# Attention and a mixture of experts on one core: k loaded two rows at a time, even rows in front of odd ones

## The chip, the core and the metric

The kernel runs on one core of a Trainium2 chip. The metric is the device time of one execution in microseconds (us), as the median of a few runs. Five engines each work through a program of their own, in order: TensorE (PE; its weight loads are shown apart as PEld), VectorE (DVE), ScalarE (ACT), GpSimd (POOL) and SyncE (SP, which issues nearly all DMA transfers). The engines meet only at semaphores. An instruction that waits holds up everything behind it in the program of its engine.

## The reference

The output is that of a block-causal attention followed by a layer of eight experts with a capacity.

```python
# q, k, v: (8 batches, 8 heads, 576 rows, 64) float32
scores = q @ k^T / sqrt(64)          # a query block of 64 rows sees key blocks up to its own
attn = softmax(scores)               # maximum taken off, masked places drop out
o = attn @ v                         # (8, 8, 576, 64)
x = o.transpose(0, 2, 1, 3).reshape(4608, 512)

logits = x @ w_gate                  # (4608, 8)
# pairs (token, expert) in falling order of logit; each expert takes at most 576 tokens
for e in range(8):
    out[mask_e] = relu(x[mask_e] @ w1[e]) @ w2[e]      # 512 -> 1024 -> 512
```

For the softmax the order of the keys in a row of scores has no meaning: the maximum and the sum run over all of them. The product with v needs the weights back in the order of the rows of v.

## The kernel before

**Stages.** The first stage is the attention with the logits, up to about 340 us of the profiled span. Then come the routing of the tokens and the experts, with PE products for the most part. The change is in the first stage alone.

**Units.** A unit n (0 to 31) is two heads of one batch, and a pair of units u = n // 2 is four heads. Loads, splits and transposes are done by pairs, scores and softmax by units. Pair 0 is handled in two halves and goes through PE transposes; pairs 1 to 15 go through DMA transposes.

**The path of k for one pair.** (1) `load_qk` (L246) brings 4 x 576 = 2304 rows of 64 float32 into the tile `kn`, 128 partitions by 18 chunks by 64: row 128c + p lies on partition p in chunk c. Each row is a run of 256 bytes in memory. There are two such tiles for k and two for q. (2) `split` makes two float16 parts of it in two halves of nine chunks each: the high part is a cast on ACT or DVE (L280, L278), the low part is the difference on POOL or DVE (L287). Both go into `k2` (`NQ=1`, one buffer). (3) A DMA transpose issued by SP (L324) turns `k2` into `kT`: partitions 0 to 63 hold one part and 64 to 127 the other, columns are the 2304 rows. (4) `swap` (L337, DVE) copies one part onto the other half of the partitions in `kS`, 1152 columns for each unit. (5) `scores` (L358, PE) multiplies: for each query block i it needs w = 64(i + 1) columns of keys. q goes the same way up to its transpose. Products of `kT` and of `kS` are added in PSUM, and the two heads of a unit go to partitions 0 to 63 and 64 to 127.

**Softmax of a unit.** The nine query blocks are taken in three groups (`GROUPS`), each in two banks of PSUM (1024 columns): group 0 holds blocks 8 and 6 with 576 and 448 columns, group 1 blocks 7, 5 and 1, group 2 blocks 4, 2, 3 and 0. DVE takes the maximum of each block (L376), ACT the exponentials with their sum into the tile `P` (L384), POOL multiplies with the reciprocal of the sum (L406). `transpose` turns `P` on PE (L431) with copies by ACT or DVE (L412, L414) into `PT`, and `values` multiplies with v (L466). A matmul writes one bank, so block 8 is cut into pieces of 512 and 64 columns.

**Other transfers of a pair.** v comes in five transfers (L261 four times, L264), together 576 KB. Results are transposed by DMA from `XT` to `XR` (L483) and written to `x` in memory (L490), 576 KB each per pair on average. So for each pair seven transfers of 576 KB go through SP: loads of k, q and v, transposes of q, k and XT, and a write.

**What sets the order.** Every function above is a generator that hands its next step to a planner (`Sched`) with an engine, a cost and the events that it waits for. The planner picks the step that can start first by its own clock, with priorities, and so fixes the program of each engine when the kernel is built. For DMAs the cost is given to `sc.dma(...)` in nanoseconds; these numbers shift the planned order on all engines, and move nothing on the chip by themselves. SP's program is in order: a transpose that waits for the low parts holds up the loads behind it.

Of the kernel before, what the change touches and what calls it, by code (L numbers as in the profile page):

```python
# [11 lines left out]
AF = mybir.ActivationFunctionType  # L12
# [148 lines left out]
class Attn:  # L161

    GROUPS = [[(8, 0), (6, 576)], [(7, 0), (5, 512), (1, 896)], [(4, 0), (2, 320), (3, 512), (0, 768)]]
# [72 lines left out]
    def load_qk(s):  # L236
        nc, sc = s.nc, s.sc
        for u in range(s.N // 2):
            b, hp = s.bh(2 * u)
            step = 2 if u else 1  # L240
            for i in range(0, 2, step):
                for nm, src in (('k', s.k), ('q', s.q)):
                    yield s.QE, 50, 'hw', ('sp', nm, 2 * (u - s.NB) + 1), ('ti', u - s.LQ)
                    if i == 0:
                        s.d[nm, u] = s.wp.tile([P, 18, s.D], F32, tag=nm + 'n', name=f"{nm}n{u}", bufs=s.NB)
                    s.ld(s.QE).dma_start(out=s.d[nm, u][:, 9 * i:9 * (i + step)],  # L246
                                         in_=src[b, 2 * (hp + i):2 * (hp + i + step)].rearrange("h s d -> (h s) d").rearrange("(c p) d -> p c d", p=P))
                    sc.dma(1638 * step, ('ld', nm, 2 * u + i))
# [3 lines left out]
    def load_v(s):  # L252
        nc, sc = s.nc, s.sc
        for u in range(s.N // 2):
# [3 lines left out]
            for h in range(4):  # L258
                if h:
                    yield s.VE, 50, 'hw'  # L260
                s.ld(s.VE).dma_start(out=t[:, 0:4, h], in_=s.v[b, 2 * hp + h, :512].rearrange("(c p) d -> p c d", p=P))  # L261
                sc.dma(728)
            yield s.VE, 50, 'hw'
            s.ld(s.VE).dma_start(out=t[:64, 4], in_=s.v[b, 2 * hp:2 * hp + 4, 512:].rearrange("h p d -> p h d"))  # L264
            sc.dma(364, ('ld', 'v', u), 625)

    def split(s, nm):
# [3 lines left out]
        for n in range(s.N):  # L271
# [4 lines left out]
            a, b = s.d[nm, u][:, 9 * i:9 * i + 9], t2[:, 9 * i:9 * i + 9]  # L276
            if sc.eng == D:
# [47 lines left out]
            sc.dma(2016 if u else 1008, ('tr', nm, n), 625, True)  # L325
# [5 lines left out]
    def swap(s):  # L331

        nc, sc = s.nc, s.sc
        for n in range(s.N):
            u, i = n // 2, n % 2
            yield D, 520, ('tr', 'k', n), ('s', 2 * (u - s.TB) + 1)
            nc.vector.tensor_copy(s.kS[u % s.TB][64:, 9 * i:9 * i + 9], s.d['kT', u][:64, 9 * i:9 * i + 9])  # L337
            sc.set(('sw', n))

    def scores(s):  # L340
        nc, sc = s.nc, s.sc
        for n in range(s.N):
            for g, G in enumerate(s.GROUPS):
                first = True
                for i, o in G:
                    w = 64 * (i + 1)
                    for a in range(0, w, 512):
                        e = min(w, a + 512)
                        yield T, 2 * ((e - a) / 2.4 + 27), Shape(2), ('tr', 'q', n), ('sw', n), 'S' if first else None
                        if first:  # L350
# [3 lines left out]
                        A, K1, K2 = [x[:, 9 * (n % 2):9 * (n % 2) + 9].rearrange("p c t -> p (c t)").rearrange("p (h t) -> p h t", h=2)  # L354
                                     for x in (s.d['qT', n // 2], s.d['kT', n // 2], s.kS[n // 2 % s.TB])]
                        for K, st in ((K1, True), (K2, False)):
                            for h in range(2):
                                nc.tensor.matmul(ps[64 * h:64 * h + 64, o + a:o + e], lhsT=A[:, h, 64 * i:64 * i + 64],  # L358
                                                 rhs=K[:, h, a:e], start=st, stop=not st)
# [3 lines left out]
                sc.add(s.softmax(n, g, tk, ps), s.PS, sc.now + 200)  # L363

# [706 lines left out]
```

## Time and profile before

| | |
|---|---|
| median of 3 runs | 801.75 us (799.38 to 802.38) |
| the profiled execution | 801.04 us, of which the span from first to last instruction is 799.3 us |
| granted PE clock, mean | 0.962 |
| busy in the span | PE 710.1 us, DVE 593.2, ACT 534.8, POOL 463.7 |
| transposes of P (L431) | 800 matmuls, 104.7 us busy |
| products with v (L466) | 792 matmuls, 97.4 us busy |
| scores (L358) | 640 matmuls of kT, 87.8 us, and 640 of kS, 80.9 us |
| exponentials (L384) | 288, 149.2 us busy |
| maxima (L376) | 288, 126.5 us busy |

The 1.8 us between the span and the time of the execution lie around the first and the last instruction. Busy times of different engines lie beside one another, so they cannot be added. A share of DMA can be over 1, since the times of packets overlap. In lists of groups the columns are line, engine, operation, what is written and read, shapes and count, then busy time in us, mean ns of one, and idle time before with its releaser.

### The profile page before, as it was taken

How to read it: one execution, taken by the hardware profiler on the slowest of the kernel's cores; microseconds unless marked ns; L12 is line 12 of the kernel's file. 1: busy time of each engine (PE TensorE's matmuls, PEld its weight loads, DVE VectorE, ACT ScalarE, POOL GpSimd, SP SyncE). 2: the span in 40 equal slices, each digit the busy share in tenths (PEclk: the TensorE clock that was granted, in tenths of full speed). 3: DMA queues.
4: the chain of work that ended last, by engine and by line, in shares of the span. 5: the costliest groups of instructions: out<-in, count | busy, mean ns of one | idle time of the engine just before them, and what ended most of it. 6: DMA issues, size and time to landing. Idle time of an engine off the chain costs nothing.

```text
span 799.3 us, 18655 instructions
## 1 busy us (share of the span) xinstructions
PE 710.1 (89%) x6301; PEld 463.5 (58%) x6301; DVE 593.2 (74%) x2487; ACT 534.8 (67%) x1450; POOL 463.7 (58%) x511
## 2 busy tenths in 40 slices
PE   5698889999988889913998999999999999999995
PEld 3565556667756657701644756647557475574752
DVE  6999879998989888788887977969687683720210
ACT  5798878989878778533845859495875847392210
POOL 5787778988888776412314337484571916773001
PEclk9989999999999999955999999999999999999998
DMA  9969999999999998544308048291945719871001
GB/s 193 180 134 194 228 185 191 216 179 212 199 181 214 200 191 168 119 96 143 128 14 296 22 161 218 86 274 43 269 121 191 166 52 257 286 159 41 21 15 44
DMA packets 286992, 125.62 MB, mean 157 GB/s; under 512 B 251568, under 2 KB 270000, under 8 KB 286896
## 3 DMA queue, kind: packets, MB, share of 16 engines
q1 hardware_dynamic: 281008, 105.55, 60.5%
q0 software_dynamic: 5888, 18.88, 7.9%
q8 instruction: 49, 0.80, 0.4%
q14 instruction: 47, 0.39, 0.2%
HBM read 71.32 MB, written 18.87 MB: 113 GB/s over the span
## 4 chain that ended last, share of the span: by engine, by line
PE 49%; DVE 22%; DMA 14%; ACT 5%; POOL 5%; issue 3%; SPq 1%; POOLq 0%; DVEq 0%; ACTq 0%
PE h L978 21%; PE y L1003 15%; DMA kT<-k 7%; DVE m L376 6%; PE psb L466 3%; PE psb L358 3%; PE psb L431 3%; POOL P L406 2%; DVE kS L337 2%; DMA raw<-in_moe_w_dram 2%; ACT P L384 2%; PE y L1007 2%; DMA xg<-x,ix 1%; DVE jk L724 1%; DVE PT L414 1%
## 5 line engine op out<-in xcount | busy, mean ns | idle before, releaser
L406 POOL TENSOR_TENSOR P<-P,m 128x576 f32<-128x576 f32 (+8 forms) x287 | 209.0, 762 | 57.3 <-DVE m L398 35.0
L978 PE MATMUL h<-X,W 128*128 128x320 f16 (+3 forms) x1536 | 194.9, 286 | 0.0
L384 ACT ACTIVATE P<-psb,m 128x576 f32<-128x576 f32 (+8 forms) x288 | 149.2, 543 | 31.3 <-DVE m L380 28.0
L978 PEld LDWEIGHTS <-W 128*128 128x128 f16 x1536 | 142.0, 98 | 42.7 <-issue 3.3
L1003 PE MATMUL y<-W,HH 128*128 128x512 f16 x512 | 152.7, 380 | 0.0
L899 POOL TENSOR_TENSOR W<-raw,W 128x1024 f16<-128x1024 f32 x56 | 118.4, 2137 | 39.1 <-ACT W L897 37.1
L376 DVE TENSOR_REDUCE m<-psb 128x1 f32<-128x576 f32 (+8 forms) x288 | 126.5, 480 | 3.5 <-PE psb L358 3.4
L431 PE MATMUL psb<-mident,P 128*128 128x128 f32 x800 | 104.7, 278 | 15.2 <-DVE XT L451 6.1
L994 POOL DMA_INDIRECT out_dram<-yo,ix x40 | 39.1, 978 | 114.9 <-ACT yo L986 79.5
L431 PEld LDWEIGHTS psb<-mident,P 128*128 128x128 f32 x800 | 86.0, 141 | 28.7 <-POOL P L406 10.3
L358 PE MATMUL psb<-kT,qT 128*64 128x512 f16 (+7 forms) x640 | 87.8, 298 | 14.9 <-DMA kT<-k 7.0
L466 PE MATMUL psb<-PT,V 128*64 128x448 f32 (+5 forms) x792 | 97.4, 388 | 1.2 <-ACT PT L412 0.9
L358 PEld LDWEIGHTS <-qT 128*64 128x64 f16 x1280 | 66.4, 113 | 53.7 <-issue 36.5
L1003 PE MATMUL y<-W,HL 128*128 128x512 f16 x256 | 97.2, 380 | 0.0
L928 POOL DMA_INDIRECT xg<-x,ix x40 | 40.4, 1010 | 95.3 <-DVE ix L866 67.6
L964 ACT ACTIVATE HH<-h 128x320 f16<-128x320 f32 (+3 forms) x128 | 52.2, 411 | 63.5 <-PE h L978 59.3
L966 DVE SCALAR_TENSOR_TENSOR HL<-h,HH 128x320 f16<-128x320 f32 (+3 forms) x128 | 56.9, 452 | 38.6 <-ACT HH L964 38.3
L358 PE MATMUL psb<-kS,qT 128*64 128x512 f16 (+7 forms) x640 | 80.9, 296 | 2.9 <-DVE kS L337 2.7
L412 ACT ACTIVATE PT<-psb 128x512 f32<-128x512 f32 (+1 forms) x151 | 75.7, 578 | 6.7 <-PE psb L431 5.0
L1003 PEld LDWEIGHTS <-HH 128*128 128x128 f16 x512 | 47.0, 98 | 53.3 <-issue 2.7
L466 PEld LDWEIGHTS psb<-PT,V 128*64 128x64 f32 x792 | 52.6, 139 | 35.7 <-issue 23.4
L893 ACT ACTIVATE raw<-raw 128x512 f32<-128x512 f32 x112 | 67.4, 626 | 7.9 <-DMA raw<-in_moe_w_dram 7.9
(200 smaller groups left out, 1067.1 us busy)
## 6 DMA issues: line engine op xcount, KB each, us to landing
raw<-in_moe_w_dram SPq DMA_DIRECT2D x64, 512.0 KB, 5.8
x<-XR SPq DMA_DIRECT2D x16, 576.0 KB, 5.8
kn<-in_k_dram SPq DMA_DIRECT2D x15, 576.0 KB, 5.2
qn<-in_q_dram SPq DMA_DIRECT2D x15, 576.0 KB, 7.8
V<-in_v_dram SPq DMA_DIRECT2D x64, 128.0 KB, 3.0
V<-in_v_dram SPq DMA_DIRECT2D x16, 64.0 KB, 2.7
xg<-x,ix POOLq DMA_INDIRECT x40, 5.1
out_dram<-yo,ix POOLq DMA_INDIRECT x40, 2.8
```

The lines of the kernel that those rows point to most:

```text
L358: nc.tensor.matmul(ps[64 * h:64 * h + 64, o + a:o + e], lhsT=A[:, h, 64 * i:64 * i + 64], rhs=K[:, h, a:e], start=st, stop=not st)
L376: nc.vector.tensor_reduce(m[:, 0, c:c + 1], ps[:, o:o + 64 * (i + 1)], axis=AX.X, op=OP.max)
L384: nc.scalar.activation(Pt[:, s.OFF[i]:s.OFF[i] + 64 * (i + 1)], ps[:, o:o + 64 * (i + 1)], AF.Exp, bias=m[:, 1, c:c + 1], scale=s.ESC, acc ...
L406: nc.gpsimd.tensor_tensor(sl, sl, m[:, 3, c:c + 1].to_broadcast([P, w]), op=OP.mult)
L412: s.nc.scalar.activation(out, in_, AF.Copy)
L431: nc.tensor.transpose(ps[:, a], s.Pb[n % s.NP][:, s.OFF[i] + 128 * j:s.OFF[i] + 128 * j + P], s.ident)
L466: nc.tensor.matmul(ps[64 * h:64 * h + 64, 64 * (i0 - b0):64 * (b1 - b0)], lhsT=vn[:, j, 2 * (n % 2) + h, :], rhs=pt[:, s.PTI[(j, i0)]:s.PT ...
L893: nc.scalar.activation(raw[:,x],raw[:,x],AF.Copy,scale=s.WS)
L899: nc.gpsimd.tensor_tensor(lw,raw,hi,op=OP.subtract)
L966: nc.vector.scalar_tensor_tensor(HL[:,f,ts],ps,0.0,HH[:,f,ts],op0=OP.max,op1=OP.subtract)
L978: nc.tensor.matmul(ps,lhsT=W[:,a,d,f*P:f*P+P],rhs=X[:,4*(d//2)+d%2+l,ts],start=(d==0 and n==0),stop=(d==3 and n==2))
L1003: if m<4: nc.tensor.matmul(ps,lhsT=Z[:,f,m*P:m*P+P],rhs=Y[:,a,f],start=(f==n==0),stop=(f==7 and n==2))
```

## The change

For pairs 1 to 15, k is loaded so that two neighbouring rows lie behind one another on a partition: row 256c + 2p + r lies on partition p in chunk 2c + r. A run in memory is then 512 bytes. `split` takes the even rows (r = 0) as its first half and the odd ones as its second, so that `kT` holds 1152 columns of even rows and then 1152 of odd rows of the four heads. `swap` copies for one unit two runs of 576 columns in place of one of 1152, and waits for the whole pair as before.

In `scores` the keys of a block are now two runs of w/2 columns, the even and the odd ones. In groups 1 and 2 one matmul takes both runs and writes them behind one another. In group 0 each run gets a matmul of its own, and even keys go to the first bank, odd ones to the second: block 6 at columns 0 to 223 and block 8 at 224 to 511 of each. For units 0 and 1, whose keys are in their old order, the two runs are the first and the second half of the columns. The maximum of group 0 runs over two pieces of w/2. The exponential reads the even and the odd key in turn and writes them in the order of the rows, so that all behind it is as before.

Besides, the costs given to the planner for DMAs are others: 2880 for a DMA transpose (2016 before), 1980 for the load of k and 2880 for that of q (3276 both), 640 and 320 for v (728 and 364), 1980 for a write of x (1638).

```diff
-    GROUPS = [[(8, 0), (6, 576)], [(7, 0), (5, 512), (1, 896)], [(4, 0), (2, 320), (3, 512), (0, 768)]]
+    GROUPS = [[(8, 224), (6, 0)], [(7, 0), (5, 512), (1, 896)], [(4, 0), (2, 320), (3, 512), (0, 768)]]
...
-                    s.ld(s.QE).dma_start(out=s.d[nm, u][:, 9 * i:9 * (i + step)],
-                                         in_=src[b, 2 * (hp + i):2 * (hp + i + step)].rearrange("h s d -> (h s) d").rearrange("(c p) d -> p c d", p=P))
-                    sc.dma(1638 * step, ('ld', nm, 2 * u + i))
+                    t, rows = s.d[nm, u][:, 9 * i:9 * (i + step)], src[b, 2 * (hp + i):2 * (hp + i + step)].rearrange("h s d -> (h s) d")
+                    if u and nm == 'k':
+                        s.ld(s.QE).dma_start(out=t.rearrange("p (c r) d -> p c (r d)", r=2), in_=rows.rearrange("(c p r) d -> p c (r d)", p=P, r=2))
+                        sc.dma(1980, ('ld', nm, 2 * u + i))
+                    else:
+                        s.ld(s.QE).dma_start(out=t, in_=rows.rearrange("(c p) d -> p c d", p=P))
+                        sc.dma(1440 * step, ('ld', nm, 2 * u + i))
...
             a, b = s.d[nm, u][:, 9 * i:9 * i + 9], t2[:, 9 * i:9 * i + 9]
+            if u and nm == 'k':
+                a = s.d[nm, u].rearrange("p (c r) d -> p r c d", r=2)[:, i]
...
-            sc.dma(2016 if u else 1008, ('tr', nm, n), 625, True)
+            sc.dma(2880 if u else 1440, ('tr', nm, n), 625, True)
...
-            nc.vector.tensor_copy(s.kS[u % s.TB][64:, 9 * i:9 * i + 9], s.d['kT', u][:64, 9 * i:9 * i + 9])
+            o, a = s.kS[u % s.TB], s.d['kT', u]
+            if u:
+                o, a = [x.rearrange("p (r c) t -> p r (c t)", r=2)[:, :, 576 * i:576 * i + 576] for x in (o, a)]
+            else:
+                o, a = o[:, 9 * i:9 * i + 9], a[:, 9 * i:9 * i + 9]
+            nc.vector.tensor_copy(o[64:], a[:64])
...
-                    for a in range(0, w, 512):
-                        e = min(w, a + 512)
-                        yield T, 2 * ((e - a) / 2.4 + 27), Shape(2), ('tr', 'q', n), ('sw', n), 'S' if first else None
+                    for r in range(1 if g else 2):
+                        yield T, 2 * ((w if g else w / 2) / 2.4 + 27), Shape(2), ('tr', 'q', n), ('sw', n), 'S' if first else None
...
-                                nc.tensor.matmul(ps[64 * h:64 * h + 64, o + a:o + e], lhsT=A[:, h, 64 * i:64 * i + 64],
-                                                 rhs=K[:, h, a:e], start=st, stop=not st)
+                                K1 = K.rearrange("p c t -> p (c t)")
+                                if n < 2:
+                                    K1 = K1[:, 1152 * n + 576 * h + (w // 2 if r else 0):][:, :w if g else w // 2]
+                                else:
+                                    j = 576 * (n % 2) + 288 * h
+                                    K1 = K1.rearrange("p (r j) -> p r j", r=2)[:, :, j:j + w // 2]
+                                    if not g:
+                                        K1 = K1[:, r]
+                                out = ps[64 * h:64 * h + 64, 512 * r + o:512 * r + o + (w if g else w // 2)]
+                                nc.tensor.matmul(out if len(K1.shape) == 2 else out.rearrange("p (r j) -> p r j", r=2),
+                                                 lhsT=A[:, h, 64 * i:64 * i + 64], rhs=K1, start=st, stop=not st)
...
+    def part(s, ps, g, i, o):
+        w = 32 * (i + 1)
+        if g == 0:
+            return ps.rearrange("p (r j) -> p r j", r=2)[:, :, o:o + w]
+        return ps[:, o:o + 2 * w].rearrange("p (r j) -> p r j", r=2)
...
-            nc.vector.tensor_reduce(m[:, 0, c:c + 1], ps[:, o:o + 64 * (i + 1)], axis=AX.X, op=OP.max)
+            nc.vector.tensor_reduce(m[:, 0, c:c + 1], ps[:, o:o + 64 * (i + 1)] if g else s.part(ps, g, i, o), axis=AX.X if g else AX.XY, op=OP.max)
...
-            nc.scalar.activation(Pt[:, s.OFF[i]:s.OFF[i] + 64 * (i + 1)], ps[:, o:o + 64 * (i + 1)], AF.Exp,
+            out, in_ = Pt[:, s.OFF[i]:s.OFF[i] + 64 * (i + 1)], s.part(ps, g, i, o)
+            out, in_ = (out.rearrange("p (r j) -> p r j", r=2), in_) if n < 2 else (out.rearrange("p (j r) -> p j r", r=2), in_.rearrange("p r j -> p j r"))
+            nc.scalar.activation(out, in_, AF.Exp,
```

SP's program around pairs 7 to 9, before. The tiles bear the number of their pair: `qT7` is the transposed q of pair 7, `kn9` the loaded k of pair 9; `XR10` is filled from `XT8`.

```order
L324 DMA_TRANSPOSE qT7_1948<-q2_7_1814 128x18x128
L324 DMA_TRANSPOSE kT7_2095<-k2_7_1913 128x18x128
L261 DMA V1_109<-in_v_dram 128x4x64 x4
L264 DMA V1_109<-in_v_dram 64x4x64
L246 DMA kn9_2173<-in_k_dram 128x18x64
L246 DMA qn9_2181<-in_q_dram 128x18x64
L483 DMA_TRANSPOSE XR10_2197<-XT8_1593 128x18x128
L324 DMA_TRANSPOSE qT8_2329<-q2_8_2128 128x18x128
L324 DMA_TRANSPOSE kT8_2369<-k2_8_2168 128x18x128
```

The same place in SP's program of the changed kernel.

```order
L332 DMA_TRANSPOSE kT7_2109<-k2_7_1902 128x18x128
L266 DMA V1_109<-in_v_dram 128x4x64 x4
L269 DMA V1_109<-in_v_dram 64x4x64
L249 DMA kn9_2231<-in_k_dram 128x9x128
L252 DMA qn9_2239<-in_q_dram 128x18x64
L332 DMA_TRANSPOSE qT7_2249<-q2_7_1891 128x18x128
L332 DMA_TRANSPOSE kT8_2308<-k2_8_2247 128x18x128
```

The load of k has runs of 128 elements in place of 64. The transpose of q of pair 7 stands in front of that of k before, and behind k's transpose, five transfers of v and the loads of pair 9 now; q of pairs 8 to 13 stands like this too, behind the load of k of two pairs later.

PE's program where the second score product of block 8 ends and the next piece begins in group 0 of a unit of pair 7, before; the product for the second head is left out.

```order
L358 LDWEIGHTS qT7_1948
L358 MATMUL psb_87<-kS1_115,qT7_1948 64x512
...
L358 LDWEIGHTS qT7_1948
L358 MATMUL psb_87<-kT7_2095,qT7_1948 64x64
...
L358 LDWEIGHTS qT7_1948
L358 MATMUL psb_87<-kT7_2095,qT7_1948 64x448
```

The same place in the changed kernel.

```order
L380 LDWEIGHTS qT7_2249
L380 MATMUL psb_87<-kS1_115,qT7_2249 64x288
...
L380 LDWEIGHTS qT7_2249
L380 MATMUL psb_87<-kT7_2109,qT7_2249 64x288
...
L380 LDWEIGHTS qT7_2249
L380 MATMUL psb_87<-kT7_2109,qT7_2249 64x224
```

Pieces of 512, 64 and 448 columns became four pieces of 288, 288, 224 and 224, each with four matmuls (two heads, `kT` and `kS`): 16 matmuls in place of 12 in group 0 of each unit, over the same 1024 columns.

More of the change, by code (lines that the diff above doesn't have):

```diff
@@ L484, in rows @@
                               in_=s.d['X', sb, hp].rearrange("p a t -> p (a t)"), transpose=True)
-            sc.dma(2016, ('xt', sb, hp), 625, True)
+            sc.dma(2880, ('xt', sb, hp), 625, True)
             if hp % 2:
```

11 lines of the change are left out of this document (5 added, 6 removed).

## The prediction, made before the changed kernel ran

> **What bounds the kernel now.** I read the chain of waits first, for which stage the change can reach, then busy times by stretch, then SP's own timeline.
>
> ```profile
> PE 49%; DVE 22%; DMA 14%; ACT 5%; POOL 5%; issue 3%; SPq 1%; POOLq 0%; DVEq 0%; ACTq 0%
> ```
>
> No single engine owns the chain. Now the stretches (columns: stretch, length, busy time of each engine with its count, granted clock, DMA share, GB/s).
>
> ```profile
> core 0: us, PE busy (x) PEld busy (x) DVE busy (x) ACT busy (x) POOL busy (x), PEclk, DMA share, GB/s
> 0.00:340.00 340.00, 298.57 (x3200) 212.84 (x3200) 296.91 (x1045) 269.95 (x829) 263.31 (x372) 0.98 0.99 187
> 340.00:799.00 459.00, 411.48 (x3101) 250.63 (x3101) 296.30 (x1443) 264.82 (x621) 200.34 (x139) 0.95 0.47 135
> 100.00:300.00 200.00, 181.47 (x1986) 129.76 (x1984) 179.84 (x636) 164.00 (x517) 166.26 (x211) 0.99 1.05 197
> 40.00:60.00 20.00, 19.38 (x188) 12.93 (x185) 18.11 (x72) 18.01 (x57) 17.66 (x22) 0.88 0.65 133
> 140.00:180.00 40.00, 38.53 (x397) 26.92 (x393) 37.16 (x140) 36.22 (x118) 36.14 (x47) 1.00 1.10 196
> 300.00:340.00 40.00, 38.34 (x460) 29.80 (x456) 30.95 (x118) 27.39 (x84) 20.98 (x34) 1.00 0.68 144
> ```
>
> The attention ends at about 340 us. From 100 to 300 us PE is busy 91% (181.5 of 200), DVE 90%, ACT 82%, POOL 83%, and DMA's share is 1.05: three resources are close to full together. In the end piece (300 to 340) PE stands at 96% and DMA has room. The experts' 459 us hold only a few swapped steps; I take them as unchanged.
>
> How full is DMA in truth? SP's timeline over one pair (start, us, instruction):
>
> ```profile
> 201.58 2.84 SPq L324 DMA_TRANSPOSE kT<-k  x1
> 204.46 2.26 SPq L261 DMA_DIRECT2D V<-in_v_dram  x4
> 206.81 0.63 SPq L264 DMA_DIRECT2D V<-in_v_dram  x1
> 207.49 0.59 SPq L246 DMA_DIRECT2D kn<-in_k_dram  x1
> 208.14 2.57 SPq L246 DMA_DIRECT2D qn<-in_q_dram  x1
> 210.75 5.39 SPq L483 DMA_TRANSPOSE XR<-XT  x1
> 216.31 2.48 SPq L324 DMA_TRANSPOSE qT<-q  x1
> 218.96 3.58 SPq L324 DMA_TRANSPOSE kT<-k  x1
> ```
>
> SP issues one transfer right behind the other, and its instructions last as long as the queue lets them: the XT transpose behind two loads takes 5.39 us, others 2.5 to 2.8. The length of a period comes from the transposes of k by themselves:
>
> ```profile
> L324 SPq DMA_TRANSPOSE kT<-k x11: 2462/2850/4312, 105.7 to 298.1; - x11
> ```
>
> Eleven starts from 105.7 to 298.1 us make ten periods of (298.1 - 105.7) / 10 = 19.24 us. The rate of packets comes from two stretches with one kind of transfer each, loads of 256-byte rows (8 to 12 us) and writes of x in 512-byte runs (139 to 141 us):
>
> ```profile
> DMA packets 3485, 0.89 MB, mean 222 GB/s; under 512 B 3485, under 2 KB 3485, under 8 KB 3485
> DMA packets 1235, 0.62 MB, mean 309 GB/s; under 512 B 42, under 2 KB 1235, under 8 KB 1235
> ```
>
> A transfer of 576 KB (589,824 bytes) takes 2.66 us at 222 GB/s and 1.91 us at 309. Three loads at 2.66, three transposes at the 2.85 us of the row above and a write at 1.91 are 18.4 us, 96% of the period. PE's share of a period is 0.907 x 19.24 = 17.5 us, DVE's 17.3. **DMA sets the pace by a little, PE and DVE stand right behind it.**
>
> **The load of k.** Runs of 512 bytes halve the packets: 1152 in place of 2304. No row shows a 512-byte load; the nearest is the write at 309 GB/s, so 1.91 in place of 2.66 us: 0.75 us less per load. Ends: 0 (the packets stay 256 bytes), and 1.33 us (a packet of 512 bytes as quick as one of 256). I take 0.75.
>
> Here the Trainium skill ("DMA: Bandwidth & Descriptors", section "Why small descriptors are slow (HBM only)") would give less: it puts a fixed 3 cycles on each packet, 11 cycles for 256 bytes, so by that rule an estimated 19 for 512, 14% less time per byte. That would be 0.36 us a load and an end near 798 us. The rows above speak against it: 222 to 309 GB/s is 28% less time per byte, though for a write.
>
> There are 15 such loads. The first three land ahead of or in the stretch from 40 to 60 us, where DMA's share falls to 0.65 in the row above: what they gain, DMA waits away. 12 x 0.75 = 9.0 us of DMA work go in paced stretches. How much reaches the end? All, if DMA alone paces; nothing, if PE does. A period of 19.24 - 0.75 = 18.5 us would need PE at 17.5 / 18.5 = 94%; the row of 140 to 180 us shows it at 96% (38.53 of 40). So it can be had, but no longer everywhere: I take three quarters, **-6.75 us**. One end is 0. The other: PE at 96% needs 17.5 / 0.96 = 18.2 us a period, so no load can bring more than 1.0 us, 15 us in all. A write stretch from 97 to 99 us comes near that, at 337 GB/s, 1.75 us a transfer, 0.91 us less than a load of 256-byte rows:
>
> ```profile
> DMA packets 1300, 0.67 MB, mean 337 GB/s; under 512 B 16, under 2 KB 1299, under 8 KB 1299
> ```
>
> **The scores.** Group 0 gets 16 matmuls for 12, over the same columns. A stretch of PE's timeline gives the price of a piece:
>
> ```profile
> 309.34 0.39 PE L358 MATMUL psb<-kT,qT 128*64 128x512 f16 x2
> 309.77 0.20 PE L358 MATMUL psb<-kT,qT 128*64 128x64 f16 x2
> 309.83 0.36 PE L358 MATMUL psb<-kT,qT 128*64 128x448 f16 x2
> 310.22 2.16 PE L466 MATMUL psb<-PT,V 128*64 128x128 f32 x14
> ```
>
> 512 columns take 0.43 us from start to start, 64 take 0.06, 448 take 0.39. From 64 to 512 that is 0.37 us for 448 columns, 0.83 ns each, so 64 columns are 0.053 and a piece costs about 0.01 us beside its columns. One more piece in 32 units is 0.3 us; for an end, 0.02 us each make 0.6. Two runs of columns in one operand add a jump; the nearest row jumps at each column, 36 elements apart, beside one with 64 columns in a row:
>
> ```profile
> L856 PE MATMUL pe<-RH,OL 128*32 128x40 f16 x288 | 7.4, 263 | 3.9 <-DVE RH L847 2.6 <-DVE RH L848 1.4
> L358 PE MATMUL psb<-kS,qT 128*64 128x64 f16 x128 | 13.7, 199 | 0.0
> ```
>
> 263 ns for 40 columns against 199 for 64: with 24 columns at 0.83 ns taken off, (263 - 179) / 40 = 2.1 ns a jump at most. 30 units with 28 matmuls of groups 1 and 2, two heads side by side, make 420 jumps one after the other: 0.9 us at most, nothing at least. In all I take **+0.3 us** for PE, ends 0 and +1.5.
>
> **Split, swap and maximum.** The split's source has runs of 64 where its target has had them already; POOL and ACT hide nothing new there. The swap must keep its speed:
>
> ```profile
> L337 DVE COPY kS<-kT 64x1152 f16<-64x1152 f16 x32 | 21.1, 668 | 13.5 <-DMA kT<-k 12.9
> L598 DVE CAST m_tok<-m_fi x1: 516/516/516, 36.4 to 36.4; 128x720 f16<-128x720 f32 x1
> ```
>
> 1152 elements in a mean of 668 ns is 0.58 ns each; a cast from runs of 36 took 0.72 ns each, so runs do not stop DVE from taking more than an element per 1.04 ns (the step of the maxima below). Cost nothing; if the swap fell to 1.04, 0.53 us in 30 units, 16 us on DVE. For the maximum over two pieces and for reads of PSUM in turn, these rows:
>
> ```profile
> L376 DVE TENSOR_REDUCE m<-psb 128x1 f32<-128x128 f32 x32 | 8.9, 278 | 0.0
> L376 DVE TENSOR_REDUCE m<-psb 128x1 f32<-128x192 f32 x32 | 11.0, 345 | 0.0
> L512 DVE TENSOR_REDUCE logits<-psb x6: 182/252/295, 131.6 to 339.8; 128x72 f32<-128x144 f32 x3, 128x32 f32<-128x64 f32 x1, 128x24 f32<-128x48 f32 x1, 128x16 f32<-128x32 f32 x1
> ```
>
> From 128 to 192 elements the maximum grows by 67 ns, 1.04 each, so 144 in a row would be 295. L512 reads 144 in pairs eight places apart and takes at most 295: DVE pays nothing for it. I cost the maximum and, by the same row, ACT's reading at nothing.
>
> **The order.** The planner's new costs move steps on all engines. q's transpose behind two loads (pairs 7 to 13) comes later by up to one load of 1.91 and one of 2.66 us; the transposes and value products of earlier units lie before its scores as cover. I take 0, with 4 us to either side.
>
> **The sum.** -6.75 + 0.3 = -6.45 us on the profiled 801.04 us: **794.6 us**. Its span is 799.3; the 1.8 around it stay. The median of the runs, 801.75, lies 0.7 above the profiled execution, well inside their spread.
>
> **The rivals.** (a) *DMA paces alone*: all 15 loads count, at 0.91 us 13.7 in all, about 787. For it speaks SP's unbroken timeline, against it PE's 96% in two stretches. (b) *No change*: the pace is that of the splits, and SP waits for POOL whatever the load takes.
>
> ```profile
> SPq L324 <- POOL P L406: 78.3, 23, 8.8
> ```
>
> SP's transposes were released by POOL 23 times, 78.3 us in all; but the queue was filled meanwhile, as DMA's share of 1.05 shows. If this paces, or the runs are cut into 256 bytes all the same (the change doing not what it says), 799 to 803. (c) *Slower: ACT's reading*. The exponential now reads an even key and an odd key in turn, w/2 or 512 places apart. No ACT row reads PSUM so. Its step now:
>
> ```profile
> L384 ACT ACTIVATE P<-psb,m 128x576 f32<-128x576 f32 x32 | 24.2, 755 | 15.0 <-DVE m L380 13.0 <-DVE m L396 1.3 <-DVE m L398 0.5
> L384 ACT ACTIVATE P<-psb,m 128x64 f32<-128x64 f32 x32 | 10.9, 341 | 0.0
> ```
>
> (755 - 341) / 512 = 0.81 ns an element. A unit has 2880 elements, a period 5760; a second step for each adds 4.7 us to ACT's 0.82 x 19.24 = 15.8, in all 20.4, or 21.3 at 96% full: 2.0 us over 19.24 in 15 periods, about 832 us. It decides from 0.45 ns an element, where ACT reaches 18.4 us. The Trainium skill ("Advanced Engine Details and Errata", section "Memory Cachelines") asks that every two consecutive PSUM elements be contiguous, which speaks for this rival; the DVE row L512 does not show such a price, and for ACT no run here shows it. (d) *Slower by the order*: if q's later transposes, 4.6 us each, held PE in those seven pairs with only half of it covered, 16 us come on top of -6.5: some 811.
>
> **How the numbers follow.** Forecast 0.52, (a) 0.12, (b) 0.19, (c) 0.09, (d) 0.08. What a measurement tells from no change is about 0.5%, 4 us. The forecast's own range is 788 to 797.7; with (a) it is faster: 0.64; (b) same: 0.19; (c) and (d) slower: 0.17. The range for 8 in 10 runs from 785 to 806: it takes in (a) and (b) and a mild form of (d), and leaves out (c).
>
> **What would show it.** Packets of 512 bytes for k, a period below 19 us between k's transposes, PE above 93% from 100 to 300 us, and the attention's end near 333 us would show the steps right. A 576-wide exponential well above 755 ns, idle time of PE in front of L380 with a DMA as its releaser, or a period still at 19.2 would show (c), (d) or (b), and the forecast wrong.

## The result, and the profile after

| | before | after |
|---|---|---|
| median of 4 runs, us | 802.04 (799.38 to 802.38) | 812.56 (810.0 to 813.54) |
| ratio to before | 1 | 1.0105 [1.0071, 1.0138] |
| profiled execution, us | 801.04 | 813.54 |
| its span, us; granted clock | 799.3; 0.962 | 811.8; 0.963 |
| last write of x issued, us | 343.9 | 351.1 |

The changed kernel is slower by 1.05%, where 0.9% faster was forecast. The clock is the same. The last write of x ends the attention; SP's timeline of the two kernels, before and then after (start, length, instruction):

```profile
343.94 1.01 SPq L490 DMA_DIRECT2D x<-XR  x2
```
```profile
351.14 1.01 SPq L522 DMA_DIRECT2D x<-XR  x2
```

7.2 of the 12.5 us between the two spans are there by the end of the attention. The other 5.3 lie in the routing and the experts, whose program is the same but for a few swapped steps. From this write to the span's end before took 455.4 us and after 460.7. In the profiles of the kernels below, taken later, that part took 458 to 467 us, and the 467 belong to a kernel as fast as before (new_path_old_order). So I lay nothing in it to the change.

The loads do what the change says. The packets of the whole program, before and then after, are 17,279 fewer, which is 15 loads of 1152, but for one:

```profile
DMA packets 286992, 125.62 MB, mean 157 GB/s; under 512 B 251568, under 2 KB 270000, under 8 KB 286896
```
```profile
DMA packets 269713, 125.64 MB, mean 155 GB/s; under 512 B 217008, under 2 KB 252720, under 8 KB 269616
```

Busy times by stretch of the changed kernel (columns as in the prediction):

```profile
core 0: us, PE busy (x) PEld busy (x) DVE busy (x) ACT busy (x) POOL busy (x), PEclk, DMA share, GB/s
0.00:340.00 340.00, 290.27 (x3211) 216.83 (x3212) 297.56 (x1036) 264.37 (x814) 270.16 (x375) 0.99 0.95 186
100.00:300.00 200.00, 178.52 (x2059) 133.98 (x2059) 178.64 (x629) 166.89 (x516) 165.14 (x208) 1.00 1.05 203
40.00:60.00 20.00, 15.04 (x174) 10.80 (x171) 18.86 (x78) 15.69 (x54) 15.47 (x21) 1.00 1.05 183
140.00:180.00 40.00, 34.41 (x350) 24.71 (x347) 29.61 (x107) 30.39 (x92) 29.57 (x38) 1.00 1.05 206
300.00:340.00 40.00, 37.45 (x394) 28.08 (x390) 33.44 (x118) 25.42 (x85) 25.78 (x37) 1.00 0.57 131
```

PE did not rise to 93% between 100 and 300 us; it stands at 89%. Up to 340 us it was busy for 290.3 us where before it was for 298.6. Some 3 of these 8.3 us are the clock, 0.99 beside 0.98. Two places stand out. From 40 to 60 us PE has 15.0 us where it had 19.4. Half of that is the clock as well: it was 0.88 before, so the 19.4 us are worth 17.1 at full clock (a score product of 512 columns took 628 ns in the half-clock parts of the attention before and 390 elsewhere). From 140 to 180 PE has 34.4 us where it had 38.5, both at full clock, with DVE at 29.6 for 37.2. Inside the second place, the ten microseconds from 150 to 160, before and then after:

```profile
150.00:160.00 10.00, 9.92 (x105) 6.70 (x104) 9.80 (x40) 10.00 (x35) 9.41 (x12) 1.00 1.25 213
```
```profile
150.00:160.00 10.00, 10.00 (x89) 7.18 (x87) 4.48 (x10) 5.68 (x14) 3.52 (x4) 1.00 1.17 203
```

PE is full, but DVE, ACT and POOL stand half empty. SP's timeline of the changed kernel says what they lack:

```profile
120.05 3.36 SPq L332 DMA_TRANSPOSE qT<-q  x1
123.51 2.73 SPq L332 DMA_TRANSPOSE kT<-k  x1
...
142.01 4.85 SPq L332 DMA_TRANSPOSE kT<-k  x1
146.92 2.24 SPq L266 DMA_DIRECT2D V<-in_v_dram  x4
149.21 0.63 SPq L269 DMA_DIRECT2D V<-in_v_dram  x1
149.89 0.59 SPq L249 DMA_DIRECT2D kn<-in_k_dram  x1
150.58 0.60 SPq L252 DMA_DIRECT2D qn<-in_q_dram  x1
151.22 7.23 SPq L332 DMA_TRANSPOSE qT<-q  x1
```

The same pairs in the kernel before:

```profile
120.14 2.77 SPq L324 DMA_TRANSPOSE qT<-q  x1
...
139.70 4.32 SPq L324 DMA_TRANSPOSE qT<-q  x1
144.12 2.84 SPq L324 DMA_TRANSPOSE kT<-k  x1
```

The transpose of q for pair 7 is issued at 151.22, 31 us after the one for pair 6; in the kernel before, the two stood at 120.14 and 139.70. Nothing in the data keeps it back so long: the low part of this q ended on POOL ten microseconds earlier.

```profile
139.96 1.28 POOL L295 TENSOR_TENSOR q<-qn,q 128x576 f16<-128x576 f32 x1
```

The transpose stands behind k's next transpose, five loads of v, one of k and one of q, because the planner put it there: from 142.01 to 151.22 SP issues these, 9.2 us. The chain of waits of this stretch (start, length, work) shows what then waits:

```profile
142.01 6.55 DMA kT<-k
148.56 2.41 POOL P L438 x4
150.96 0.21 SPq L252
151.18 0.04 issue
151.22 9.29 DMA qT<-q
160.51 0.04 issue
160.55 1.08 PE psb L380 x16
161.64 0.02 issue
161.66 1.30 DVE m L405 x2
```

The scores begin at 160.55, the moment q's transpose lands. PE had value products and transposes of earlier units to fill the time; DVE, ACT and POOL had no scores to work on. One more line of the same timeline is worth seeing: the load of q is accepted in 0.60 us, where in the kernel before it took 1.57 to 3.61 between 96 and 300 us. What it gains, the transpose behind it waits: 7.23 us. The run new_path_old_order below has the order of before and shows the two side by side, before and then with the new loads:

```profile
150.74 2.28 SPq L246 DMA_DIRECT2D qn<-in_q_dram  x1
153.12 5.28 SPq L483 DMA_TRANSPOSE XR<-XT  x1
```
```profile
149.55 0.64 SPq L252 DMA_DIRECT2D qn<-in_q_dram  x1
150.30 8.12 SPq L517 DMA_TRANSPOSE XR<-XT  x1
```

Its nine loads of q in that stretch took 0.60 to 0.83 us, and the six transposes of XT behind such loads 6.14 to 8.12, where before they took 4.81 to 6.35. SP's time moved from the load to the next instruction in the queue.

What the change promised for the data came true. The stretch from 16.3 to 17.3 us holds loads of k alone; the one from 18 to 20 us, but for one packet, loads of q in 256-byte rows:

```profile
DMA packets 670, 0.34 MB, mean 342 GB/s; under 512 B 4, under 2 KB 670, under 8 KB 670
```
```profile
DMA packets 1696, 0.45 MB, mean 225 GB/s; under 512 B 1695, under 2 KB 1695, under 8 KB 1695
```

At these rates 576 KB take 1.72 and 2.62 us, 0.9 us apart. The costly groups show no price for the new order of the elements (busy us and mean ns behind the first bar):

```profile
L416 ACT ACTIVATE P<-psb,m 128x576 f32<-128x576 f32 x32 | 24.0, 751 | 16.6 <-DVE m L409 13.3 <-PE psb L498 2.5 <-PE psb L380 0.4
L405 DVE TENSOR_REDUCE m<-psb 128x1 f32<-128x576 f32 x32 | 24.0, 750 | 4.0 <-PE psb L380 2.3 <-POOL P L438 1.6
L350 DVE COPY kS<-kT x32: 454/712/1525, 9.8 to 302.1; 64x1152 f16<-64x1152 f16 x32
```

The last line has the fastest, the median and the slowest copy. The median of 712 ns (455 before) is not a price of the two runs: with the order of before (new_path_old_order) it is 454, and with the new order and the old path (old_path_new_order) it is 571.

### The profile page after: what moved, and what is told of

Its sections match the earlier page's. It is cut to its first block, busy times and chain, and to the rows that moved or that the text cites. A ratio compares the mean times of both kernels' runs of the same rounds, so it can differ in the third digit from the quotient of the medians.

```text
span 811.8 us, 18957 instructions
## 1 busy us (share of the span) xinstructions
PE 712.0 (88%) x6429; PEld 473.8 (58%) x6429; DVE 597.3 (74%) x2493; ACT 531.6 (65%) x1439; POOL 470.5 (58%) x516
## 4 chain that ended last, share of the span: by engine, by line
PE 46%; DVE 24%; DMA 10%; ACT 8%; POOL 5%; issue 4%; SPq 0%; POOLq 0%; DVEq 0%; ACTq 0%
PE h L1010 20%; PE y L1035 15%; DVE m L405 7%; ACT P L416 4%; DMA raw<-in_moe_w_dram 3%; PE psb L463 3%; DMA kT<-k 3%; PE psb L498 3%; POOL P L438 3%; DVE PT L446 2%; DMA qT<-q 2%; PE y L1039 2%; PE psb L380 2%; DVE kS L350 2%; DMA xg<-x,ix 1%
## 5 line engine op out<-in xcount | busy, mean ns | idle before, releaser
L463 PEld LDWEIGHTS psb<-mident,P 128*128 128x128 f32 x800 | 88.0, 143 | 34.4 <-POOL P L438 11.3
L380 PE MATMUL psb<-kT,qT 128*64 128x288 f16 (+8 forms) x704 | 88.8, 280 | 20.0 <-ACT P L416 16.5
L380 PEld LDWEIGHTS <-qT 128*64 128x64 f16 x1408 | 75.6, 110 | 50.5 <-issue 33.2
L380 PE MATMUL psb<-kS,qT 128*64 128x288 f16 (+8 forms) x704 | 81.6, 277 | 0.0
```

The source lines that it names most:

```text
L380: nc.tensor.matmul(out if len(K1.shape) == 2 else out.rearrange("p (r j) -> p r j", r=2), lhsT=A[:, h, 64 * i:64 * i + 64], rhs=K1, start= ...
L463: nc.tensor.transpose(ps[:, a], s.Pb[n % s.NP][:, s.OFF[i] + 128 * j:s.OFF[i] + 128 * j + P], s.ident)
```

## The experiments

Each ratio stands against runs of the kernel before on the same chip, with its 95% interval. Chips differ (the kernel before had medians from 802 to 811 us on them), so ratios are compared across batches and not times. Expectations in us are on the scale of the kernel before at 802 us; 1% is 8 us.

### The path without the order, the order without the path

The change does two things that can be had apart: it moves k's data in another way, and it gives the planner other numbers. The planner's numbers changed in two ways too: the costs of DMAs, and the count of steps for the scores of group 0 (four planned steps where there were three). So four kernels.

**new_path_old_order**: the changed kernel with the planner's old numbers and three steps, so that all engines run the steps in the order of the kernel before.

```diff
-                        sc.dma(1980, ('ld', nm, 2 * u + i))
+                        sc.dma(1638 * step, ('ld', nm, 2 * u + i))
...
-            sc.dma(2880 if u else 1440, ('tr', nm, n), 625, True)
+            sc.dma(2016 if u else 1008, ('tr', nm, n), 625, True)
...
-                    for r in range(1 if g else 2):
-                        yield T, 2 * ((w if g else w / 2) / 2.4 + 27), ...
+                    for z in range(0, w, 512):
+                        e = min(w, z + 512)
+                        yield T, 2 * ((e - z) / 2.4 + 27), ...
+                        for r in ([0] if g else [z // 512] if w > 512 else [0, 1]):
```

> The data path of the changed kernel (loads of k in 512-byte runs, scores in two runs, exponentials that read in turn), while the planner is given the costs and steps of before, so that each engine's program has the order of before. Theory A (the new order costs, the data path itself gains): 795 us, between 790 and 800, with SP's period below 19 us. Theory B (the data path costs, by two-run operands or shared banks): 808 us or more, with longer score products or longer waits of PE for them.

Measured: 0.9994 [0.9966, 1.0022]. Last write of x at 343.3 us (before 343.9); ten periods from 105.61 to 297.22, 19.16 us each (before 19.24). The whole new way of the data, loads that are a third shorter included, moves the time by nothing that can be measured. Both theories miss: the path neither gains what A had it gain nor costs what B had it cost.

**old_path_new_order**: the kernel before, with the new costs and four planned steps.

```diff
-            sc.dma(2016 if u else 1008, ('tr', nm, n), 625, True)
+            sc.dma(2880 if u else 1440, ('tr', nm, n), 625, True)
...
-                    for a in range(0, w, 512):
-                        e = min(w, a + 512)
-                        yield T, 2 * ((e - a) / 2.4 + 27), ...
+                    for r in range(1 if g else 2):
+                        yield T, 2 * ((w if g else w / 2) / 2.4 + 27), ...
+                        a = 512 * r
+                        e = min(w, a + 512)
...
-                            for h in range(2):
+                            for h in range(2 if a < e else 0):
```

> The data path of before in the order of the changed kernel on every engine. Theory A: 815 to 820 us, the changed kernel without what its loads gain, and the transpose of q of pair 7 some 10 us later than before, as in the changed kernel. Theory B: 802 us, as before.

Measured: 1.0122 [1.0072, 1.0172], some 10 us, less than theory A's 13 to 18 but its way. The attention ends at 354.5 us, 10.6 later than before, and pair 7's q is transposed at 155.77, 16 us later. The order alone is the whole loss. It has the same two holes at the same places, without one new packet:

```profile
40.00:60.00 20.00, 15.44 (x146) 9.38 (x144) 19.55 (x76) 14.73 (x49) 15.34 (x19) 1.00 1.18 193
140.00:180.00 40.00, 34.36 (x325) 23.57 (x319) 27.45 (x97) 28.27 (x87) 26.71 (x34) 0.96 1.01 202
150.00:160.00 10.00, 10.00 (x88) 7.16 (x87) 4.79 (x11) 5.68 (x13) 3.84 (x6) 1.00 1.06 199
```

**costs_only**: the kernel before with the new costs of DMAs (all of them: `1638` to `1980` for k and for x, to `1440` for q, `2016` to `2880`, `728` and `364` to `640` and `320`), and its own three steps.

> The kernel before with the planner's new DMA costs and nothing else; the scores of group 0 are planned in their old pieces. Theory A1 (the new DMA costs make the order that costs): 808 to 818 us, with q's transposes behind the loads of two pairs later again. Theory A2 (planning group 0 in four pieces makes it): 800 to 804 us. Theory B: 802 us.

Measured: 0.9898 [0.9861, 0.9935], **faster than the kernel before by 1%**. Its attention ends 8 us earlier, and PE is busier between 100 and 300 us:

```profile
335.80 1.01 SPq L490 DMA_DIRECT2D x<-XR  x2
```
```profile
100.00:300.00 200.00, 186.26 (x2056) 131.74 (x2052) 184.69 (x662) 164.95 (x522) 172.35 (x217) 0.99 1.07 202
```

None of the three theories had this (794 us). In these orders the new costs alone do good, and with the fourth step as well the order is bad.

**q_before_loads**: the changed kernel, with the loads of a pair planned behind the transposes of both q and k of two pairs earlier, where it had been k's alone. Then q's transpose can't fall behind two loads.

```diff
-            if nm == 'k':
+            s.ti[u] = s.ti.get(u, 0) + 1
+            if s.ti[u] == 2:
                 sc.ev['ti', u] = sc.now
```

> The changed kernel, with one rule more for the planner: the loads of a pair wait until both transposes of two pairs earlier are issued, not only that of k. SP's program is the same up to pair 7 and then has q's transposes ahead of the loads again. Theory A with the place of q's transposes as the cause: 798 to 803 us, the 10 us between pairs 6 and 7 gone. Theory A with another part of the order as the cause: 809 us or more. Theory B: 809 us or more.

Measured: 1.0069 [1.0035, 1.0103]. Pair 7's transpose is issued at 147.06 and the hole is mostly filled, on ACT the least:

```profile
140.00:180.00 40.00, 36.95 (x401) 27.48 (x397) 35.59 (x128) 31.55 (x96) 35.06 (x43) 1.00 1.02 201
150.00:160.00 10.00, 10.00 (x117) 7.06 (x117) 8.04 (x31) 7.43 (x19) 7.92 (x8) 1.00 1.12 212
```

Yet of 1.05% only 0.36 is gone, about a third, and the intervals overlap, so the runs don't show that even this third is real. The time, some 807 us by the ratio, lies between the two theories. q's late transpose is at most a part of the loss.

The exponentials say more. There are 288 in each trace, 18 for a pair, and the start of the nth tells how far the attention has come (us of the profiled executions; the 126th is the last of pair 6, the 144th of pair 7, the 234th of pair 12):

| | 126th | 144th | 234th | 288th |
|---|---|---|---|---|
| before | 151.8 | 167.8 | 265.1 | 327.3 |
| after | 146.5 | 175.8 | 277.0 | 330.9 |
| old_path_new_order | 147.3 | 179.5 | 280.1 | 334.3 |
| q_before_loads | 146.5 | 168.7 | 269.7 | 331.7 |

The changed kernel is 5.3 us ahead of the kernel before at the end of pair 6, for all its thin stretch from 40 to 60 us, and 8.0 behind at the end of pair 7: the late q costs 13 us there. q_before_loads has 7 of these back at that place and none of them at the 288th. From the 234th to the 288th the changed kernel regains 8 us. Each order, that of before too, wins and loses such stretches, and what counts is what is left at the end.

### What sets the pace, then

Four kernels that take work from one resource each, and one pair that completes the first table.

**before_no_v**: the kernel before with the loads of v for the first three pairs only.

```diff
+                if u < 3:
                     s.ld(s.VE).dma_start(out=t[:, 0:4, h], ...)
```

> The kernel before in its own order, where v is loaded for the first three pairs alone and later pairs use what lies in the buffers: 13 transfers of 576 KB fewer, 2.66 us of DMA work by 256-byte packets each, so 35 us of DMA work in all are left out. Theory D (DMA sets the pace in the attention): 20 to 35 us faster. Theory P (the pace is set by the engines in their planned order, and DMA follows): 0 to 5 us faster.

Measured: 0.9928 [0.9894, 0.9963], 5.8 us, just above the 5 of theory P and far from D. The trace shows DMA's share falling from 1.05 to 0.91 while PE rises by only three us in 200:

```profile
100.00:300.00 200.00, 184.40 (x2034) 133.13 (x2030) 183.25 (x647) 167.86 (x527) 170.06 (x216) 1.00 0.91 170
```

13 x 2.66 = 35 us of transfers out, 5.8 us won: 0.17 us for each us. By this rate the 15 x 0.9 = 13.5 us that the loads of k got shorter are worth an estimated 2.2 us, or 0.28%, inside the interval of new_path_old_order.

**before_one_product**: one of the two products of each score left out.

```diff
-                        for K, st in ((K1, True), (K2, False)):
+                        for K, st in ((K1, True),):
```

> The kernel before in its own order, with the score products of kS left out, which is half of the score products: 640 matmuls, heads side by side, about 0.9 ns a column, some 38 us of PE work in all. Theory D: 0 to 5 us faster. Theory P with PE as the engine that counts: 15 to 35 us faster. If neither this nor the run without loads of v moves the time much, the chain runs through DVE, ACT and POOL.

Measured: 0.9961 [0.9941, 0.9982], 3.1 us. PE's busy time up to 340 us fell from 298.6 to 274.4, by 24 us (at a clock of 0.95 for 0.98, so by an estimated 32 us of full-clock work):

```profile
0.00:340.00 340.00, 274.39 (x2563) 187.55 (x2563) 297.52 (x1063) 269.30 (x830) 265.03 (x373) 0.95 0.99 189
```

**before_short_max** and **before_short_mult**: the maximum over 64 columns of each block; the product with the reciprocal over 64 columns of each.

```diff
-            nc.vector.tensor_reduce(m[:, 0, c:c + 1], ps[:, o:o + 64 * (i + 1)], axis=AX.X, op=OP.max)
+            nc.vector.tensor_reduce(m[:, 0, c:c + 1], ps[:, o:o + 64], axis=AX.X, op=OP.max)
```
```diff
+            w = 64
             sl = Pt[...]
```

> The kernel before in its own order, where the maximum of each block of scores is taken over its first 64 columns alone: 288 maxima at 213 ns in place of a mean of 480, 77 us of DVE work left out. If DVE sets the pace of the attention: 25 to 60 us faster. If no single engine does, and the chain winds through all of them in the planned order: 5 to 20 us faster.

> The kernel before in its own order, where only the first 64 columns of each block of weights are multiplied with the reciprocal of their sum, so the rest stays unscaled: 287 products at 312 ns in place of a mean of 762, some 130 us of POOL work left out. If POOL sets the pace, by the low parts that stand behind these products: 25 to 60 us faster. If no single engine does: 5 to 20 us faster.

Measured: 0.9953 [0.9925, 0.9982], 3.8 us, less than either case had it, and 0.9901 [0.9871, 0.9931], 8 us, inside the 5 to 20. The same stretch shows 67 us less on DVE for the one and 120 less on POOL for the other:

```profile
0.00:340.00 340.00, 299.09 (x3203) 214.11 (x3203) 230.34 (x1063) 268.54 (x830) 264.37 (x373) 0.97 1.00 189
```
```profile
0.00:340.00 340.00, 297.57 (x3205) 211.56 (x3205) 285.73 (x1082) 269.80 (x834) 143.10 (x374) 0.98 1.02 191
```

**None of the four paces the attention by itself**: each us taken away brings 0.06 to 0.17 us, in an order that was planned for the full work. Taking work from ACT, or from two engines at once, was not tried. Nor was a shorter transpose: between 100 and 300 us the chain of waits before has transposes of k in 25.2% of the time, more than any other group (the maxima of L376 have 17.5%), and none of these runs changes a transpose.

**new_path_three_steps**: the changed kernel with its new costs and three planned steps, so in the order of costs_only. **four_steps_only**: the kernel before, its own costs, four planned steps. The edits are halves of those above.

> The data path of the changed kernel and its new DMA costs, while the planner plans group 0 in the three steps of before; each engine's program has the order of the run with new costs alone (0.990 of before). Theory A with three parts that add (data path 0, new DMA costs -1%, planning four steps +2%): 0.988 to 0.992 of before. If the shorter loads of k count once the order is good: 0.980 to 0.985. If the data path and the new costs do not go together: 1.00 or more.

> The kernel before with its own DMA costs and its own score pieces, but group 0 planned in four steps as in the changed kernel. Theory A1 (four steps by themselves make a bad order): 1.010 to 1.020 of before. Theory A2 (only the four steps together with the new DMA costs do): 0.99 to 1.005. Theory A3 (any other order is a throw of dice around this one): no forecast, between 0.985 and 1.02.

Measured: 0.9929 [0.9903, 0.9955], at the edge of the first case, and 1.0097 [1.0064, 1.0129], at the edge of A1. With all that was run, by order and by path:

| order | old path | new path |
|---|---|---|
| old costs, three steps | 1 | 0.9994 [0.9966, 1.0022] |
| new costs, three steps | 0.9898 [0.9861, 0.9935] | 0.9929 [0.9903, 0.9955] |
| new costs, four steps | 1.0122 [1.0072, 1.0172] | 1.0105 [1.0071, 1.0138] |
| old costs, four steps | 1.0097 [1.0064, 1.0129] | not run |

Along each row the path makes no difference that the intervals can tell. The differences lie down the columns. And the numbers don't add: the new costs bring -1.0% and the four steps +1.0%, both together +1.2%. four_steps_only has no hole from 150 to 160 us, and its pair 7 transposes q at 144.5:

```profile
150.00:160.00 10.00, 8.95 (x84) 5.90 (x84) 8.76 (x30) 9.67 (x29) 8.11 (x11) 1.00 0.88 183
```

It is as slow as the changed kernel nonetheless. The late q can't be the cause of that.

### Is it the start?

In the orders above, the first DMA transpose of k is issued at 29.6 to 30.8 us with four steps, and at 25.5 to 26.3 with three. If this start were the loss, four steps for the first two units alone would cost it, and four steps for all the others would not.

```diff
+                four = n > 1 and not g        # three_then_four; n < 2 in four_then_three
...
+                    for z in ([0, 512] if four else range(0, w, 512)):
```

> Data path and DMA costs of the changed kernel; group 0 is planned in three steps for units 0 and 1 and in four from unit 2 on. If the start makes the bad order (the split of pair 1's k behind three exponentials, its transpose issued near 30 us in every order with four steps and near 25.5 in every order with three): 0.990 to 0.998 of before, with that transpose near 25.5 us. If four steps make a bad order in the steady part: 1.005 to 1.015.

> Data path and DMA costs of the changed kernel; group 0 is planned in four steps for units 0 and 1 and in three from unit 2 on. If the start makes the bad order: 1.004 to 1.012 of before, with the transpose of pair 1's k near 30 us. If four steps make a bad order in the steady part: 0.990 to 0.998. If any change of the planner's numbers throws the order anew: no forecast, between 0.985 and 1.015.

Measured: three_then_four 0.9993 [0.9964, 1.0023], its first transpose at 25.83; four_then_three 0.9904 [0.9869, 0.994], its first at 29.68. The late start is there in the faster of the two: **it is not the cause**. The hole at 40 to 60 us goes with it: PE has 16.0 us of 20 there in four_then_three and 16.9 in costs_only, and both are 1% faster than before. three_then_four fits neither case: four steps from unit 2 on are not bad by themselves.

### Is it a meaning or a throw?

The planned cost of a score step ends in `+ 27`, nanoseconds by the planner's clock. 26 or 28 mean the same step; they only fall differently where two steps are nearly equal. If the orders differ by chance, this alone moves the time.

```diff
-                        yield T, 2 * ((w if g else w / 2) / 2.4 + 27), ...
+                        yield T, 2 * ((w if g else w / 2) / 2.4 + 26), ...     # 28 in the other
```

> The kernel before, where the planner counts 26 ns in place of 27 beside the columns of a pair of score products: a number that means nothing to the chip. Theory O (the order is a throw, and 1% either way lies in it): anything from 0.985 to 1.015 of before, not within 0.995 to 1.005 in at least two of the four kernels of this kind. Theory S (four steps in the plan are bad in a systematic way): 0.995 to 1.005.

> The kernel before with 28 ns in place of 27. Theory O: anything from 0.985 to 1.015 of before. Theory S: 0.995 to 1.005.

> The changed kernel with 26 ns in place of 27 in the planner. Theory O: anything from 0.985 to 1.015 of before, and so perhaps faster than before. Theory S: 1.005 to 1.015, as the changed kernel.

> The changed kernel with 28 ns in place of 27 in the planner. Theory O: anything from 0.985 to 1.015 of before. Theory S: 1.005 to 1.015, as the changed kernel.

Measured, against the unedited kernel before:

| | + 26 | + 27 | + 28 |
|---|---|---|---|
| before | 1.0001 [0.9971, 1.0032] | 1 | 1.0024 [0.9997, 1.005] |
| after | 1.0000 [0.9966, 1.0033] | 1.0105 [1.0071, 1.0138] | 1.0039 [1.0007, 1.0071] |

(One of the ten executions of before_step28 took 2267.8 us, for no reason that I know, and is left out.) Neither expectation holds as it was worded. All four lie within 0.995 to 1.005, so the orders aren't thrown as widely as theory O had it. But the changed kernel's loss of 1% is gone with one number 1 ns lower, and more than half of it with that number 1 ns higher, so the loss isn't a lasting trait of the change, as theory S had it. The orders do differ widely: up to 360 us SP has 177 instructions with a transfer, and with 26 in the changed kernel 69 of the places, from 61 us on, hold another kind of transfer; with 26 in the kernel before it is 49, at the same time. With 26 the stretch with the hole is full:

```profile
140.00:180.00 40.00, 38.00 (x404) 29.08 (x403) 37.37 (x134) 33.57 (x108) 32.77 (x42) 1.00 1.03 202
```

The stretch behind it is thinner instead: from 180 to 220 us DVE has 31.0 us there, where the kernel before has 37.3.

## Why the prediction was wrong

The forecast was -6.45 us; the measured ratio is worth +8.4. Of the 15 us between them, some 6 belong to the pace and 9 to the order (1.0105 against the 0.9994 of the same path in the old order). Both terms failed.

**The pace.** The step that failed first is "DMA sets the pace by a little, PE and DVE stand right behind it", and with it "I take three quarters, -6.75 us". The path alone brought 0.06% less time, +-0.28, so at most some 2.7 us. before_no_v shows that DMA does not pace: 35 us of transfers out of the same stage bring 5.8. That a resource's transfers fill 96% of a period, and that SP issues one behind the other, showed that it was nearly full; it didn't show that the others would go faster if it were not. The same holds for PE (24 us out, 3.1 won), DVE (67, 3.8) and POOL (120, 8.0). The reading that fits these runs is that with in-order programs on five engines work is held up now by one, now by another, and that to relieve one leaves all the others; it is inferred, since no run relieved two. The size that I gave as an end of the range, 0, lies inside the interval.

**The order.** "I take 0, with 4 us to either side" is the term that decided the sign. Held against the same path, the order measured +1.22% (old path), some 10 us; the new costs with three planned steps measured -1.0%, some 8 us to the other side. Both lie outside the 4 us. The working behind the term also left something out: it let q's transpose come later by "one load of 1.91 and one of 2.66 us", 4.6 in all, where the order shown under The change has k's transpose and five transfers of v ahead of it too. SP took 9.2 us for all of these at pair 7, and q's transpose came 11.5 us later than before.

**The load of k.** Right: runs of 512 bytes came at 342 GB/s beside 225 for 256, 0.9 us a load where 0.75 was taken. The rule of the Trainium skill ("DMA: Bandwidth & Descriptors", "Why small descriptors are slow (HBM only)") would have it at an estimated 14% less time per byte; the two stretches show 34%, and the measurement decides.

**Scores, swap, maximum, exponential.** Right as far as they could be told: the copy's fastest is 454 ns (445 before), the widest maximum 750 (749), the widest exponential 751 (755). With the old order the path as a whole cost nothing that shows, four more matmuls a unit included. Rival (c) falls with the 751 ns. The Trainium skill ("Advanced Engine Details and Errata", "Memory Cachelines") asks for two consecutive PSUM elements side by side for best throughput; ACT's reading in turn does not bear that out, with its 751 ns beside 755 in a row.

**The rivals.** (a) falls with before_no_v. (b) had the right size for the data, but not for its reason: the splits' engine, relieved of 120 us, gave back 8. (d) gave 811, near the 812.56, and its mechanism is there to see, q's transpose behind two loads and a hole after it. But the agreement of the number is luck: its sum holds -6.5 us for the loads, which did not come, and 16 us for seven pairs, where pair 7 alone lost 13 and the end of the attention gave 8 back. With the hole mostly filled 1.0069 remains, and four_steps_only loses as much without it. Also the shape was another than (d) had it: PE was covered until the scores could start, and DVE, ACT and POOL were what stood idle.

**What stays open.** Which places of the order carry the loss. The start and the late q have been tried; the pair with 26 doesn't narrow it down, since its two orders differ nearly throughout. Nor is it settled whether four steps are a little worse on average: of the six orders with four steps (from the start or from unit 2 on) none is faster than before beyond its interval, and of the five with three steps there none is slower. So "the change is slower" means here: this order, out of several that the same change could have had, is a bad one. The change with three planned steps is faster than the kernel before by 0.7%, and nothing in that shows a gain of the path, since the kernel before with the same numbers gains 1.0%. The fastest run is that one, costs_only at 0.9898, with four_then_three (0.9904) level with it.

## What to carry to other kernels

A busy share of 90% on several resources doesn't say which of them paces, or that any does: before costing a saving at its full size, look for what else is within some per cent, or take the work out of one and measure what a us is worth (here 0.06 to 0.17 us). Where a planner fixes the order from a table of costs, an edit of the data path and its edit of the table are two changes: time each without the other, and a few neighbours of the table as well, before judging either. One number of the planner, changed by one nanosecond, gave another order and moved this kernel by 1%, as much as the whole edit cost.

## What the runs showed of the hardware

Two runs of 256 bytes made into one of 512 raised a load from 225 to 342 GB/s, more than the writes at 309 and 337 had let expect. DVE's copy of float16 kept its speed with two runs of 576 elements in place of one of 1152 (a median of 454 against 455 ns in the same order), and ACT read PSUM in turn from two places 512 elements apart as fast as in a row (751 against 755 ns). A queue's gain can also show on the wrong instruction: in the same order, with the load of k shorter, the load of q behind it was accepted in 0.60 to 0.83 us for 1.57 to 3.61, and the transposes behind that took 6.14 to 8.12 for 4.81 to 6.35.
